# Two attention blocks with their gradients: head groups of four instead of five, with their out and dx products spread over 26 ticks

## The chip, the cores and the metric

The kernel runs on one core of one Trainium2 chip. The metric is the device time of one execution in microseconds; lower is better. The kernel before was timed three times: 1642.14, 1643.09 and 1643.6 us, so the median is 1643.09 us. Besides its time, an execution leaves a profile: a record of every instruction on the engines TensorE (PE; its weight loads are listed apart as PEld), VectorE (DVE), ScalarE (ACT), GpSimd (POOL) and SyncE (SP).

## What is computed

The reference runs two independent attention blocks A and B and concatenates their outputs; then it takes the gradient of all ten inputs for a given `grad_out`. The kernel returns the output and the ten gradients. One block is, with 8 batches of 96 queries, model width 640, 32 heads of 128, and 512 cached keys and values per batch and head, all bf16:

```python
q = (x @ wq).reshape(B, Sq, H, Dh).transpose(0, 2, 1, 3)
scores = jnp.einsum("bhqd,bhkd->bhqk", q, k_cache) * (Dh ** -0.5)
p = softmax(scores, axis=-1)
o = jnp.einsum("bhqk,bhkd->bhqd", p, v_cache)
out = o.transpose(0, 2, 1, 3).reshape(B, Sq, H * Dh) @ wo
```

For the change, two products matter. `out` is a sum over all 32 heads of (attention output of the head) times (that head's 128 rows of `wo`). The gradient `dx` is likewise a sum over heads of (gradient of the head's queries) times (that head's columns of `wq`, transposed). Both have 768 rows (8 x 96) and 640 columns.

## The kernel before, in words

**Ticks.** The work of block A and then of block B is cut into ticks: one tick for one batch of one head, so 8 ticks for a head, 256 for a block, 512 in all. `build_block` (line 54) does not emit instructions directly. It puts closures into a list with a tick and a slot (`em.add(tick, slot, fn)`), and at the end `Emitter.run` sorts the list by tick and slot and calls them. A scheduler below it takes the instructions in about this order and moves one only where a buffer or an input is not there yet. In the trace a tick can be found by its one product S_ps (L298).

**What a tick holds.** The stages of one batch of one head are spread over several ticks, so that a tick holds different stages of neighbouring batches (offsets in `OFF`, line 45): the scores S_ps (L298), their row maximum negm on VectorE (L300), the exponential E_sb on ACT (L310), its reciprocal row sum rinv (L320), P_sb on GpSimd (L329), four transposes of P and of dS (L365, L346), the attention output and the gradient of the queries into one bank x_ps (L359, L340), which ACT empties (OD, L375, and PT_sb, L378), and dV, dP and dK (L389, L417, L432), of which ACT empties dV and dK, and VectorE takes dP into dS (L421).

**What a head holds.** Once per head there are projections and weight gradients at fixed ticks of the head (`HK`, line 46): `pB` (L206 and after) transposes the head's slices of wo and wq on TensorE and copies them out as woT_h (ACT) and wqT_h (VectorE, L160); `pC` makes Q and dO (q_ps, L243); `pD` transposes them (n_ps, L258; dOnat_h and Qnat_h, L160); `qA` (nat_ps, L455), `qB` (dwo_ps, L469) and `qD` (dwq_ps, L490, once for two heads) make the gradients of wo and wq.

**What a group of heads holds.** The products for `out` and `dx` are made per group of heads: `gU` (L514) accumulates in one PSUM bank over the heads of the group, for one of 6 row tiles of 128 and one of two column pieces (512 and 128 wide), and then the bank is emptied. Here this is called a unit: 24 units for a group, 12 for `out` and 12 for `dx`, each with as many matmuls as the group has heads. The first group of a block writes its units into two f32 accumulators in SBUF, out_acc and dx_acc, by ACT (L157). All groups between add to them on VectorE (L518 for out, L520 for dx). The last group adds and writes the result as bf16, which is then stored.

**Where the units stand.** `cLg` is the last tick of the group. The 12 units of `out` begin 7 ticks after it and are spread evenly over `gs0` ticks; those of `dx` begin `gs0` + 7 ticks after it and are spread over `gs1`. Before, both are 9 for a group of five, 7 for a group of four, and 3 for the group of two. Block A has groups of 5, 5, 5, 5, 4, 4, 4 heads, block B of 5, 5, 5, 5, 5, 5, 2.

**Buffers that matter.** PSUM has one pool of 8 banks ("bank") for all tiles whose names end in `_ps`. wqT_h has 7 buffers (`HG` + 2, with `HG` = 5), and each is needed until the dx units of its group are done. OD, which holds the attention outputs and query gradients of the heads, has 7 places, and wo_h has 8 buffers.

Of the kernel before, what the change touches and what calls it, by code (L numbers as in the profile page):

```python
# [47 lines left out]
GSPREAD0 = 9  # L48
PRIO_OFF = 2000
GSPREAD1 = 9  # L50
# [3 lines left out]
def build_block(tc, em, tick0, blk, x, kc, vc, wq, wo, g_all, out_all, dx, dk, dv, dwq, dwo, ident, ones, pools, HG=6, first=True, groups=None):  # L54
# [12 lines left out]
    HG = min(HG, H)  # L67
    if groups is None:
        n_g = -(-H // HG)
        groups = [H // n_g + (1 if i < H % n_g else 0) for i in range(n_g)]  # L70
# [125 lines left out]
    def pA2(h):  # L196
        def f():
            wo_h = hst.tile([128, D], BF16, name="wo_h", bufs=HG + 3)
            ld = nc.sync.dma_start(wo_h[:], wo[h * 128:(h + 1) * 128, :])
            if not (first and h == 0):  # L200
                pinned(ld)
            HS[(blk, h)]["wo_h"] = wo_h
        return f
# [352 lines left out]
    def k_on_pe(h, b):  # L556
        return h == 0 or (first and h == 1)

    SX = pools["SX"]
    for g in range(NG):  # L560
        h0 = GH0[g]
        for hh in range(groups[g]):
            h = h0 + hh
            c0t = tick0 + h * B
            if not (first and h == 0):
                em.add(c0t + HK["pA"], SLOTS["LOAD"] + 1.7, pA(h))
                em.add(c0t + HK["pA2"], SLOTS["LOAD"] + 1.7, pA2(h))
            em.add(c0t + HK["pB"], SL_HEAD, pB(h))
            fh = first and h == 0
            p0, p1, d1, d0, late = HK["pC0"], HK["pC1"], HK["pD1"], HK["pD0"], 0  # L570
            if fh:
                p1, d1, d0, late = [3, 3], 3, 4, 7
            elif h == 0:
                p0, p1, d1, d0, late = [-2, 2], [0, 3], 3, 4, 7
            for si in range(NTS):
                em.add(c0t + p0[min(si, 1)], SL_HEAD, pC(h, 0, si))
                em.add(c0t + p1[min(si, 1)], SL_HEAD + late, pC(h, 1, si))
            em.add(c0t + d1, SL_HEAD + (8 if late else 0), pD(h, 1))
            em.add(c0t + d0, SL_HEAD, pD(h, 0))
            for b in range(B):  # L580
                ct = c0t + b
                if b % NB == 0:
                    em.add(tick0 - 12 if first and h == 0 and b == 0 else ct + OFF["ldk"], SLOTS["LOAD"], c_ld(h, b, "K", 7))
                    em.add(ct + OFF["ldv"], SLOTS["LOAD"], c_ld(h, b, "V", 6))
                    if not k_on_pe(h, b):
                        em.add(ct + OFF["kt"], SLOTS["LOAD"] + 1, c_xt(h, b, "KT", 4))
                    em.add(ct + OFF["vt"], SLOTS["LOAD"] + 1, c_xt(h, b, "VT", 4))
                if k_on_pe(h, b):
                    em.add(ct + 2, SLOTS["S1"], c_s1(h, b))
                em.add(ct + OFF["s2"], SLOTS["S2A"], c_s2a(h, b))  # L590
                em.add(ct + OFF["s2"], SLOTS["S2B"], c_s2b(h, b))
                em.add(ct + OFF["s3"], SLOTS["S3A"], c_s3a(h, b))
                em.add(ct + OFF["s3"], SLOTS["S3B"], c_s3b(h, b))
                em.add(ct + OFF["s5"], SLOTS["S5B"], c_s5b(h, b))
                if b % 2 == 1:
                    em.add(ct + OFF["s4"] + 1, SLOTS["LOAD"] + 1.5, c_st(h, b, "v"))
                    em.add(ct + OFF["s7"] + 1, SLOTS["LOAD"] + 1.5, c_st(h, b, "k"))
                em.add(ct + OFF["s4"], SLOTS["S4"], c_s4(h, b))
                for i, o in enumerate(("s8", "s7", "s5", "s4")):
                    SX.setdefault(ct + OFF[o], [None] * 4)[i] = (blk, h, b)  # L600
                em.add(ct + OFF["s6"], SLOTS["S6"], c_s6(h, b))
                em.add(ct + OFF["s7"], SLOTS["S7"], c_s7(h, b))
            hk = HK if first or h < H - 1 else dict(HK, qA0=13, qB=[14, 15], qA1=16, qD=[(19, 0, 2), (19, 2, 4), (19, 4, 5)])
            em.add(c0t + hk["qA0"], SL_HEAD, qA(h, 0))
            for di in range(len(wsplits)):
                em.add(c0t + hk["qB"][di], SL_HEAD + 1, qB(h, di))
            em.add(c0t + hk["qB"][-1] + 1, SLOTS["LOAD"] + 1.6, qB_st(h))
            em.add(c0t + hk["qA1"], SL_HEAD, qA(h, 1))
            for (k_, c_lo, c_hi) in hk["qD"]:
                if c_lo < DC and h % 2 == 1:  # L610
                    em.add(c0t + k_, SL_HEAD + 2, qD(h, c_lo, min(c_hi, DC)))
            if h % 2 == 1:
                em.add(c0t + hk["qD"][-1][0] + 1, SLOTS["LOAD"] + 1.6, qD_st(h))
        cLg = tick0 + (h0 + groups[g] - 1) * B + B - 1
        gs0 = max(3, (GSPREAD0 * groups[g]) // HG)
        gs1 = max(3, (GSPREAD1 * groups[g]) // HG)
        if not first and g == NG - 2:
            gs0, gs1 = 9, 9
        if g == 0:
            em.add(cLg + OFF["s5"] - 2, SL_LOAD, setup_acc)  # L620
        subs = [(0, t, gi) for t in range(TT) for gi in range(len(gsplits))] + [(1, t, gi) for t in range(TT) for gi in range(len(gsplits))]
        n_out = TT * len(gsplits)
        for i, (which, t, gi) in enumerate(subs):
            if which == 0:
                tk = cLg + OFF["s5"] + 2 + (i * gs0) // n_out
            else:
                tk = cLg + OFF["s8"] + 2 + gs0 - 3 + ((i - n_out) * gs1) // n_out
            em.add(tk, SL_GRP, gU(g, which, t, gi))
            if g == NG - 1 and gi == len(gsplits) - 1:
                em.add(tk + 1, SLOTS["LOAD"] + 1.6, gU_st(which, t))  # L630
# [3 lines left out]


def _kernel_impl(tc, A_x, A_k_cache, A_v_cache, A_wq, A_wo, B_x, B_k_cache, B_v_cache, B_wq, B_wo, grad_out,
           out_0, out_1, out_2, out_3, out_4, out_5, out_6, out_7, out_8, out_9, out_10, HG=5, slots=None, off=None, hk=None, ev=None, gspread=None, groupsA=None, groupsB=(5, 5, 5, 5, 5, 5, 2)):
    global GSPREAD0, GSPREAD1
    nc = tc.nc
    if slots:  # L640
        SLOTS.update(slots)
    if off:
        OFF.update(off)
    if hk:
        HK.update(hk)
    if ev:
        EV.update(ev)
    if gspread:
        GSPREAD0, GSPREAD1 = gspread
    with ExitStack() as ctx:  # L650
        P = lambda **kw: ctx.enter_context(tc.tile_pool(**kw))
        cst = P(name="gconst", bufs=1)
        ident = cst.tile([128, 128], BF16, name="ident")
        make_identity(nc, ident[:])
        ones = cst.tile([128, 1], BF16, name="ones")
        nc.vector.memset(ones[:], 1.0)
        warm = cst.tile([128, 128], BF16, name="warm")
        nc.vector.memset(warm[:], 1.0)
        pools = dict(
            const=P(name="const", bufs=1),  # L660
            ps=P(name="ps", bufs=8, space=PSUM),
            kvp=P(name="kv", bufs=11),
            wk=P(name="wk", bufs=3),
            hd=P(name="hd", bufs=2),
            hst=P(name="hst", bufs=HG + 2),
            grp=P(name="grp", bufs=1),
            stp=P(name="stp", bufs=5),
        )
        warm_ps = pools["ps"].tile([128, 128], F32, name="warm_ps", tag="bank")
        for _ in range(32):  # L670
            nc.tensor.matmul(warm_ps[:], warm[:], warm[:], start=True, stop=True)
        pools["SX"] = {}
        pools["XP"] = {}
        pools["OD"] = pools["const"].tile([128, 2, HG + 2, A_x.shape[0] * A_x.shape[1]], BF16, name="OD", bufs=1)
        pools["HS"] = {}
        pools["CS"] = {}
        em = Emitter()
        t_next = 13
        for blk, args in enumerate(((A_x, A_k_cache, A_v_cache, A_wq, A_wo, grad_out, out_0, out_1, out_2, out_3, out_4, out_5),
                                    (B_x, B_k_cache, B_v_cache, B_wq, B_wo, grad_out, out_0, out_6, out_7, out_8, out_9, out_10))):  # L680
            H_ = args[1].shape[1]
            if blk == 0:
                grps = groupsA
            else:
                grps = groupsB
            t_next = build_block(tc, em, t_next, blk, *args, ident, ones, pools, HG=HG, first=(blk == 0), groups=grps)
        for tk, (k8, k7, k5, k4) in pools["SX"].items():
            em.add(tk, SLOTS["S8"], pools["c_s8"](tk, k8, k7))
            em.add(tk, SLOTS["S5"], pools["c_s45"](tk, k8, k5, k4))
        em.run()  # L690
# [64 lines left out]
```

## Time and profile before

| | |
|---|---|
| time, median of 3 | 1643.09 us (1642.14 to 1643.6) |
| profiled execution: time, span | 1643.09 us, 1641.3 us |
| around the span | 1.8 us |
| TensorE clock granted | 1.000 |
| VectorE, GpSimd busy | 1268.2 us, 526.7 us |
| HBM traffic | 161.09 MB read, 159.12 MB written |
| matmul records | 21048 |
| group products (L514) | 1536 |

The span reaches from the first to the last instruction of the execution; the time has some 1.8 us around it. A row of a group of instructions reads: line, engine, operation, tile written and tiles read, shapes, count | busy us, mean ns of one | idle time of the engine just before them, and what ended it. A row of the waits reads: engine and line that waited, whom it waited for, us in total, number of times, the longest. A row of a timeline reads: start in us, length in us, instruction, and in brackets the idle time before it. Since matmuls overlap in the array, the length of a matmul's record (219 ns for 128 columns) is longer than its distance to the next one.

### The profile page before, as it was taken

To read this page: it belongs to the slowest core of one execution; us is meant where nothing else is said; L and a number is where in the kernel's file an instruction comes from. 1 tells how busy PE (TensorE), PEld (TensorE's weight loads), DVE (VectorE), ACT (ScalarE), POOL (GpSimd) and SP (SyncE) were. 2 spreads that over 40 slices of the span, in tenths; PEclk is the share of its full clock that TensorE was granted. 3 is DMA by queue.
4 is the path that set the end of the run, shared out by engine and by line. 5 is a ranking of instruction groups with operands and counts; after the bars stand their busy time and mean duration, and the time that the engine had idled before them with its cause. 6 is when DMAs were issued, how large, how long until landed. Compare 5 with 4: busy or idle time off the path is not lost.

```text
span 1641.3 us, 55280 instructions
## 1 busy us (share of the span) xinstructions
PE 1621.3 (99%) x21048; PEld 1289.1 (79%) x21048; DVE 1268.2 (77%) x2856; ACT 1388.7 (85%) x3518; POOL 526.7 (32%) x1034
## 2 busy tenths in 40 slices
PE   8999999999999999999999999999999999999999
PEld 7887787787787787877878877877877877877876
DVE  6886677778787787788878867878778778777777
ACT  7999897898798797988869998978977978987975
POOL 2333232333233232333323332323322322332332
PEclk9999999999999999999999999999999999999999
DMA  9999999999999999999999999999999999999994
GB/s 266 289 282 294 269 291 291 271 271 292 260 272 293 279 274 271 264 281 285 297 284 292 293 289 279 284 298 260 291 291 258 280 277 282 283 292 259 281 276 146
DMA packets 875626, 454.96 MB, mean 277 GB/s; under 512 B 548192, under 2 KB 875360, under 8 KB 875360
## 3 DMA queue, kind: packets, MB, share of 16 engines
q1 hardware_dynamic: 875360, 451.43, 112.4%
q8 instruction: 165, 2.70, 0.7%
q14 instruction: 101, 0.83, 0.1%
HBM read 161.09 MB, written 159.12 MB: 195 GB/s over the span
## 4 chain that ended last, share of the span: by engine, by line
PE 81%; ACT 10%; DVE 4%; issue 3%; DMA 2%; SPq 0%; POOL 0%; ACTq 0%; DVEq 0%; POOLq 0%
PE q_ps L243 13%; PE o_ps L514 12%; PE dwq_ps L490 6%; PE dP_ps L417 6%; PE dK_ps L432 6%; PE dV_ps L389 5%; PE S_ps L298 5%; PE dst_ps L346 5%; PE dwo_ps L469 4%; PE x_ps L365 4%; PE x_ps L359 4%; PE x_ps L340 4%; ACT E_sb L310 3%; ACT dK_sb L435 2%; PE n_ps L258 2%
## 5 line engine op out<-in xcount | busy, mean ns | idle before, releaser
L329 POOL TENSOR_SCALAR P_sb<-E_sb,rinv 96x512 bf16<-96x512 bf16 x512 | 352.5, 689 | 1087.9 <-DVE rinv L320 1053.6
L310 ACT ACTIVATE E_sb<-S_ps,negm 96x512 bf16<-96x512 f32 x512 | 354.8, 693 | 119.2 <-DVE negm L300 116.8
L421 DVE SCALAR_TENSOR_TENSOR dS_sb<-dP_ps,dl_ps,P_sb 96x512 bf16<-96x512 f32 x512 | 383.6, 749 | 48.9 <-PE dl_ps L419 40.2
L435 ACT ACTIVATE dK_sb<-dK_ps 128x512 bf16<-128x512 f32 x512 | 306.9, 599 | 97.5 <-PE dK_ps L432 96.5
L300 DVE TENSOR_REDUCE negm<-S_ps 96x1 f32<-96x512 f32 x512 | 347.7, 679 | 44.3 <-PE S_ps L298 42.1
L392 ACT ACTIVATE dV_sb<-dV_ps 128x512 bf16<-128x512 f32 x512 | 315.8, 617 | 0.0
L378 ACT ACTIVATE PT_sb<-x_ps 128x384 bf16<-128x384 bf16 x512 | 257.5, 503 | 0.0
L514 PEld LDWEIGHTS <-OD 128*128 128x128 bf16 x1536 | 135.7, 98 | 103.3 <-issue 1.3
L389 PE MATMUL dV_ps<-dOnat_h,P_sb 96*128 96x128 bf16 x2048 | 197.9, 219 | 0.6 <-DVE dOnat_h L160 0.6
L432 PE MATMUL dK_ps<-Qnat_h,dS_sb 96*128 96x128 bf16 x2048 | 197.8, 219 | 0.0
L417 PE MATMUL dP_ps<-VT,dOT_h 128*96 128x512 bf16 x512 | 195.4, 382 | 0.7
L298 PE MATMUL S_ps<-KT,QT_h 128*96 128x512 bf16 x488 | 184.7, 379 | 3.9 <-ACT E_sb L310 2.7
L407 POOL TENSOR_TENSOR prod<-OD,dOT_h 128x96 bf16<-128x96 bf16 x512 | 185.6, 362 | 8.8 <-ACT OD L375 8.2
L348 DVE COPY dST_sb<-dst_ps 128x384 bf16<-128x384 bf16 x512 | 177.2, 346 | 14.0 <-PE dst_ps L346 13.2
L320 DVE RECIPROCAL rinv<-rowsum 96x1 f32<-96x1 f32 x512 | 80.0, 156 | 138.8 <-ACT E_sb L310 134.8
L346 PE MATMUL dst_ps<-ident,dS_sb 96*128 96x96 bf16 x2048 | 171.8, 206 | 4.3 <-ACT PT_sb L378 3.6
L375 ACT ACTIVATE OD<-x_ps 128x192 bf16<-128x192 f32 (+1 forms) x515 | 172.5, 335 | 3.4 <-PE x_ps L340 3.4
L359 PE MATMUL x_ps<-PT_sb,V_sb 128*128 128x96 bf16 x2048 | 172.2, 206 | 0.5 <-ACT PT_sb L378 0.5
L365 PE MATMUL x_ps<-ident,P_sb 96*128 96x96 bf16 x2048 | 171.7, 205 | 0.6 <-POOL P_sb L329 0.3
L340 PE MATMUL x_ps<-dST_sb,K_sb 128*128 128x96 bf16 x2048 | 170.7, 206 | 0.0
L340 PEld LDWEIGHTS <-K_sb 128*128 128x128 bf16 x2048 | 133.7, 98 | 37.1
L514 PE MATMUL o_ps<-wo_h,OD 128*128 128x128 bf16 (+1 forms) x768 | 141.0, 299 | 0.0
(75 smaller groups left out, 3051.9 us busy)
## 6 DMA issues: line engine op xcount, KB each, us to landing
out_dram<-dV_sb SPq DMA_DIRECT2D x256, 256.0 KB, 3.9
out_dram<-dK_sb SPq DMA_DIRECT2D x256, 256.0 KB, 3.6
K_sb<-in_A_k_cache_dram SPq DMA_DIRECT2D x128, 256.0 KB, 4.1
V_sb<-in_A_v_cache_dram SPq DMA_DIRECT2D x128, 256.0 KB, 4.1
K_sb<-in_B_k_cache_dram SPq DMA_DIRECT2D x128, 256.0 KB, 4.2
V_sb<-in_B_v_cache_dram SPq DMA_DIRECT2D x128, 256.0 KB, 4.0
out_dram<-dwo_sb SPq DMA_DIRECT2D x64, 160.0 KB, 3.2
out_dram<-dwq_sb SPq DMA_DIRECT2D x32, 320.0 KB, 3.8
```

Source lines behind the costliest of these rows:

```text
L298: nc.tensor.matmul(S_ps[:], hs["QT_h"][:, tok], st["KT"], start=True, stop=True)
L300: nc.vector.tensor_reduce(negm[:], S_ps[:], axis=AX.X, op=ALU.max, negate=True)
L310: nc.scalar.activation(E_sb[:], st["S_ps"][:], ACT.Exp, bias=st["negm"][:], scale=1.0, accum_out=rowsum[:])
L329: pinned(nc.gpsimd.tensor_scalar(P_sb[:], st["E_sb"][:], st["rinv"][:], 0.0, op0=ALU.mult, op1=ALU.add))
L340: nc.tensor.matmul(dQT_ps, st["K_sb"][:, c, :], st["dST_sb"][:, c * Sq:(c + 1) * Sq], start=(c == 0), stop=(c == KC - 1))
L389: nc.tensor.matmul(dV_ps[:, c * 128:(c + 1) * 128], P_sb[:, c * 128:(c + 1) * 128], hs["dOnat_h"][:, b * 128:(b + 1) * 128], start=True, s ...
L392: nc.scalar.activation(SB[(blk, h, b // 2, "v")][:, b % 2], dV_ps[:], ACT.Identity, scale=1.0)
L417: nc.tensor.matmul(dP_ps[:], hs["dOT_h"][:, tok], st["VT"], start=True, stop=True)
L421: nc.vector.scalar_tensor_tensor(dS_sb[:], dP_ps[:], dl_ps[:, 0:1], st["P_sb"][:], op0=ALU.subtract, op1=ALU.mult)
L432: nc.tensor.matmul(dK_ps[:, c * 128:(c + 1) * 128], dS_sb[:, c * 128:(c + 1) * 128], hs["Qnat_h"][:, b * 128:(b + 1) * 128], start=True, s ...
L435: nc.scalar.activation(SB[(blk, h, b // 2, "k")][:, b % 2], dK_ps[:], ACT.Identity, scale=1.0)
L514: nc.tensor.matmul(o_ps[:], src[:, t * 128:(t + 1) * 128], rhs, start=(hh == 0), stop=(hh == groups[g] - 1))
```

## The change

Block A is cut into eight groups of four heads, and block B into 5, 5, 4, 4, 4, 4, 4, 2. The units of a group of four are spread over 13 and 13 ticks (the one but last group of block B keeps 9 and 9, as before), those of a group of five over 9 and 9, those of the group of two over 3 and 3. `HG` stays 5, so all buffers stay as they are. The matmuls are the same in number and shape except that each unit of a group of four accumulates over four heads.

```diff
         cLg = tick0 + (h0 + groups[g] - 1) * B + B - 1
-        gs0 = max(3, (GSPREAD0 * groups[g]) // HG)
-        gs1 = max(3, (GSPREAD1 * groups[g]) // HG)
+        gs0, gs1 = {2: (3, 3), 4: (13, 13)}.get(groups[g], (9, 9))
         if not first and g == NG - 2:
             gs0, gs1 = 9, 9
...
-           out_0, out_1, out_2, out_3, out_4, out_5, out_6, out_7, out_8, out_9, out_10, HG=5, slots=None, off=None, hk=None, ev=None, gspread=None, groupsA=None, groupsB=(5, 5, 5, 5, 5, 5, 2)):
+           out_0, out_1, out_2, out_3, out_4, out_5, out_6, out_7, out_8, out_9, out_10, HG=5, slots=None, off=None, hk=None, ev=None, gspread=None, groupsA=(4,) * 8, groupsB=(5, 5, 4, 4, 4, 4, 4, 2)):
```

## The prediction

> **What bounds the kernel now.** I read the busy rows first, then the chain of work that ended last.
>
> ```profile
> PE 1621.3 (99%) x21048; PEld 1289.1 (79%) x21048; DVE 1268.2 (77%) x2856; ACT 1388.7 (85%) x3518; POOL 526.7 (32%) x1034
> ...
> PE 81%; ACT 10%; DVE 4%; issue 3%; DMA 2%; SPq 0%; POOL 0%; ACTq 0%; DVEq 0%; POOLq 0%
> ```
>
> TensorE is never idle for long, and 81% of the chain is its own work; ACT, the next, has 10%. But matmuls overlap, so busy time does not tell how much of it is lost. For that I took from the trace the distance from each matmul's start to the next one's. Its median is nearly constant for a form: 216 ns for 512 columns, 56 ns for 128, 42 to 43 ns for 96. What exceeds the median of the same tile and form I call lost: 54.1 us in all. The other 1587 us of the 1641.3 us span are nearly all matmul work, which the change moves but does not add to. So at stake is the 54.1 us, less jitter: the quietest of the 511 stretches between two S_ps products (one per tick, numbered from 0) still show some 19.5 ns each, 10 us in all.
>
> Where is the rest lost? In the timeline of TensorE two places look like this:
>
> ```profile
> 205.40 0.30 PE L469 MATMUL dwo_ps<-g_nat,Onat 128*128 128x320 bf16 x1
> 205.86 0.38 PE L298 MATMUL S_ps<-KT,QT_h 128*96 128x512 bf16 x1 [0.16 <-ACT E_sb L310]
> ...
> 300.84 0.39 PE L389 MATMUL dV_ps<-dOnat_h,P_sb 96*128 96x128 bf16 x4
> 301.33 0.42 PE L417 MATMUL dP_ps<-VT,dOT_h 128*96 128x512 bf16 x1
> ```
>
> First: a 320-column product, 0.135 us long by its median, is followed 0.46 us later, because ACT's exponential came late: 0.32 us lost. This is in a tick without group products. Second: four 56 ns products take 0.49 us, 0.27 us too long. Here dP_ps waited until VectorE had emptied dOnat, so for a PSUM bank. This is in a tick with dx products.
>
> By stretches, without the 19.5 ns of jitter: **(a)** the 283 stretches without group products hold most of it. At the same places of the 16 ticks of a head pair they lose the same each time, by number modulo 16: 0.197 us at 15, 0.318 at 0, 0.329 at 3, often 0.195 at 6 and 0.1 to 0.17 at 7. **(b)** In the out half of a group of five nothing is lost. **(c)** In its dx half it is 0.97 us: 0.44 and 0.26 in two stretches that hold two products each, 0.13 in one, the rest in crumbs of 0.035. **(d)** The three groups of four that end the first block (7+7 ticks) lose almost nothing while they run.
>
> The reason for (a) is in busy time by stretch of time, first a group of four, then ticks without:
>
> ```profile
> core 0: us, PE busy (x) PEld busy (x) DVE busy (x) ACT busy (x) POOL busy (x), PEclk, DMA share, GB/s
> 610.30:665.00 54.70, 54.53 (x674) 41.80 (x672) 43.82 (x100) 41.40 (x106) 16.00 (x32) 1.00 1.10 260
> 665.00:702.50 37.50, 37.29 (x520) 31.03 (x517) 29.34 (x67) 35.65 (x92) 13.57 (x27) 1.00 1.19 279
> ```
>
> ACT is busy 35.65 of 37.5 us (95%) without group products and 76% with them. Group products are TensorE work that costs ACT nothing; in their ticks ACT catches up.
>
> The reason for (c) is a wait that VectorE shows nine times:
>
> ```profile
> DVE wqT_h L160 <- PE o_ps L514: 3.7, 9, 0.4
> ```
>
> There are 7 buffers of wqT_h. Where the head seven later comes before the dx products of the group are done, its transposes (pB) wait in PSUM. In the built order of before this happens in nine groups of five: one bank of eight is taken for 10 stretches, a second for 3. (d) has no such wait, and no loss.
>
> **The change, part by part.** *It moves* TensorE work only: 1536 group products before and after. In the built order 228 stretches have some before, 361 after. Before, up to 10 products of five heads (two units) fall in one stretch; after, a group of four gives one unit to each of 24 ticks, 32 ticks apart. A pair of units (512 and 128 columns) is 4 x (216 + 56) = 1.09 us, so 0.54 us per tick against 0.907 (5 x 272 x 12 over 18).
>
> *It adds* VectorE work: 16 groups instead of 14, each 24 evictions, and all added ones add to the accumulators: 48.
>
> ```profile
> L520 DVE SCALAR_TENSOR_TENSOR dx_acc<-o_ps,dx_acc 128x512 f32<-128x512 f32 x60 | 41.4, 690 | 30.6 <-PE o_ps L514 30.5
> ...
> L520 DVE SCALAR_TENSOR_TENSOR dx_acc<-o_ps,dx_acc 128x128 f32<-128x128 f32 x60 | 16.6, 277 | 0.0
> ```
>
> 24 x (690 + 277) = 23.2 us, so VectorE goes from 1268 to 1291 us, 79% of the span. The cover is its 373 us of idle time. Per group tick it gets 0.48 us more than its base of 2.2 us (1268 less 240 adds at 0.48 us, over 512), 2.7 of about 3.2 us, 84%. If that cover were gone, the bounds are 0 and the 23.2 us; I take 0 on its own, and its effect on banks below.
>
> *Stretches without products.* After a group of four only 7 are left out of 32, at 12, 13, 14, 15, 0, 1, 2 of 16, and the next group's first product comes behind the place of loss at 3. From (a): 0.197 + 0.318 + 0.329 = 0.84 us per group.
>
> *The dx halves.* By the built order of after, 14 groups hold a bank (9 stretches, a second one 2), always at the phase of (c). Bounds: nothing, as in (d), and 0.97 us, as in (c). The two stretches with two units lost 0.70 of the 0.97; they now have one, as where 0.035 to 0.15 was lost. I take 0.5 us.
>
> The Trainium skill (Perfetto Trace Analysis, Matmul Optimizations) asks that all 8 PSUM banks be used; that speaks against this change, and (b) against (c) agrees with it. By that rule alone the longer holding, 154 stretches against 117, would cost the full 0.97 us per group, which is the second case below.
>
> *First group of block one.* Its evictions are on ACT (24 of 0.28 to 0.60 us, 10.6 us). ACT's average of 2.67 us per tick (1388.7 less 21 us, over 512) becomes 3.11 in 3.2, as tight as in (a). 24 ticks at (a)'s mean excess, 0.1 us or less, give 0 to 2.4; I take 1.5 us.
>
> *Queues.* SP's stores of block one's out and dx move to other ticks; each waits for VectorE (3.8 us in four waits now). Behind them on SP stand K and V loads that are issued four to five ticks ahead, over 12 us, so nothing. wqT_h copies that wait: 14 x 0.41 us on VectorE instead of 9, inside its idle time. Nothing moves on POOL. The end: the last but one group has four heads, so 9 products fewer (1.2 us) follow the last S_ps; they are done earlier, no gain.
>
> *The sum*, lost time without jitter:
> - stretches 32 to 255: 15.4 now; after 7 x (0.84 + 0.5) + 1.5 = 10.9; -4.5
> - 256 to 287 (block start, whose own waits stay): 2.7, after about 2.2; -0.5
> - 288 to 367, two groups of five: unchanged
> - 368 to 495: 9.2; after 4 x 1.34 = 5.4; -3.8
>
> Together -8.8 us. The profiled execution took 1643.09 us (span 1641.3 and 1.8 around it), which is also the median of the runs. Forecast: **1634.3 us**.
>
> **Rivals.** *Full price for held banks.* The dx half loses 0.97 us as before, in every group. Then 7 x 1.81 + 1.5 = 14.2, the block start 2.7, 4 x 1.81 = 7.2: -3.2 us, **1640 us**. For: the phase is the same, and a smaller PE share per tick leaves ACT less time. Against: losses sit in the two-unit stretches. 0.2.
>
> *Slower: VectorE late.* A tick now has only 0.54 us of group products to cover 0.48 us of adds; before 0.907 to cover 0.64. If VectorE's adds then hold o_ps banks and delay negm in every group tick, the out halves lose 0.97 us too: 11 x (0.84 + 1.94) + 1.5 + 3.7 = 35.8 against 27.3: +8.5, **1652 us**. It decides from where the two halves together lose 1.3 us per group ((27.3 - 1.5) / 12 - 0.84). For: ACT already waits for negm.
>
> ```profile
> ACT E_sb L310 <- DVE negm L300: 116.8, 190, 2.1
> ```
>
> Against: (b) and (d) lose nothing with denser adds. 0.15.
>
> *No loss in the dx halves*, as in (d), and none in the first group: -8.8 - 6 - 1.5, **1627 us**. For: one unit per tick. 0.1.
>
> *It moves nothing* because ACT's lag is only made up elsewhere: 1643 us. Against: (a) repeats to some ns at fixed places. 0.05. That the products don't spread is excluded by the built order.
>
> **How the numbers follow.** The forecast has 0.5 and 1629 to 1639 as its own range. The measurement of this kernel tells about 0.2% (3.3 us) from no change. Faster: 0.5 + 0.1 and a third of the 0.2 that falls below 1639.8, so 0.66. Same: the rest of that and 0.05, so 0.19. Slower: 0.15. The range leaves out the VectorE case and reaches from the case without loss to beyond full price, with the first group's 2.4: 1626 to 1646.
>
> **What would show it.** Right: TensorE's busy time and products as before, VectorE near 1291 us; lost time near 45 us; the losses at 6 and 7 gone and those at 15, 0, 3 once per group of four; wqT_h waiting 14 times. Wrong: matmul gaps behind out_acc or negm in out halves (VectorE case), or 0.2 to 0.4 us gaps at dP_ps, dwq_ps and S_ps in every dx half (bank case).

## The result and the profile after

The changed kernel takes 1646.08 us (median of 17 runs, 1645.5 to 1647.11) against 1642.92 us (17 runs) for the kernel before on the same chips: ratio 1.0019, interval 1.0012 to 1.0027. It is slower by 3.2 us. The forecast was 1634.3 us, and 1646.08 lies just outside the range of 1626 to 1646. The profiled execution took 1646.16 us with a span of 1644.4 us.

The first two lines of the page that answer to those shown of before, busy time and the shares of the chain of work:

```profile
PE 1614.1 (98%) x20850; PEld 1287.4 (78%) x21048; DVE 1295.0 (79%) x2904; ACT 1393.2 (85%) x3518; POOL 528.5 (32%) x1034
...
PE 81%; ACT 10%; DVE 4%; issue 4%; DMA 1%; POOL 0%; SPq 0%; ACTq 0%; DVEq 0%; POOLq 0%
```

The picture is that of before: TensorE bounds. VectorE has 48 instructions more and 26.8 us more work. One number misleads: 20850 matmuls against 21048. The 21048 weight loads are all there, and the built program has as many matmuls as before; 198 matmul records are missing from this trace, 133 of o_ps and 65 of q_ps, all 512 columns wide. Whoever takes distances from start to start must put them back at 216 ns each first, or counts 42.8 us of work as lost. I matched the records to the program's order. Then the work, each matmul at the median of its form, is 1587.2 us in both kernels, and the lost time is **53.1 us before and 56.1 us after**: 3.0 of the 3.2 us. (Here a form is told apart by its inputs too; by the tile written alone, as in the prediction, the 53.1 us are 54.1.)

By stretches between two S_ps, without 19.5 ns of jitter each, in us:

| stretches | before | forecast | after |
|---|---|---|---|
| 32 to 63 (first group in after) | 2.2 | 2.8 | 1.8 |
| 64 to 255 | 12.7 | 8.0 | 15.7 |
| 256 to 287 | 2.6 | 2.2 | 3.0 |
| 288 to 367 (unchanged groups of five) | 6.2 | 6.2 | 5.3 |
| 368 to 495 | 8.9 | 5.4 | 9.5 |

A middle group of four repeats every 32 stretches, at most places to a few nanoseconds. Its parts (mean of four groups, stretches 96 to 223) are what the study is about:

| part, number of the stretch modulo 32 | forecast | after |
|---|---|---|
| without products, and the first one (29 to 3) | 0.84 | 0.92 |
| out half (4 to 16) | 0 | 0.75 |
| dx half (17 to 28) | 0.5 | 0.75 |

The ticks without products cost about what was forecast, and look as before. First busy time in a group's 25 ticks and then without products, then the place where a 320-column product is followed 0.46 us later:

```profile
core 0: us, PE busy (x) PEld busy (x) DVE busy (x) ACT busy (x) POOL busy (x), PEclk, DMA share, GB/s
307.70:390.80 83.10, 81.88 (x1038) 64.70 (x1049) 66.01 (x147) 68.03 (x173) 25.77 (x51) 1.00 1.13 280
390.80:411.00 20.20, 19.80 (x283) 16.38 (x283) 17.21 (x40) 19.66 (x52) 8.00 (x16) 1.00 1.11 265
```

```profile
403.85 0.30 PE L469 MATMUL dwo_ps<-g_nat,Onat 128*128 128x320 bf16 x1
404.31 0.38 PE L298 MATMUL S_ps<-KT,QT_h 128*96 128x512 bf16 x1 [0.16 <-ACT E_sb L310]
```

ACT is 97% busy without products, 82% with them. VectorE has 79% in the group's ticks; no engine beside TensorE is full there. The waits:

```profile
ACT E_sb L310 <- DVE negm L300: 139.3, 212, 2.0
...
DVE wqT_h L160 <- PE o_ps L514: 5.4, 14, 0.5
```

wqT_h waits in 14 groups, as the built order said. And ACT waits 22.5 us longer for negm. The new loss stands in the out half, at the ticks numbered 7 modulo 8 (0.34 us at 7, 0.44 at 15). Timelines of TensorE, VectorE and ACT there:

```profile
321.17 0.38 PE L298 MATMUL S_ps<-KT,QT_h 128*96 128x512 bf16 x1
...
322.68 0.38 PE L417 MATMUL dP_ps<-VT,dOT_h 128*96 128x512 bf16 x1
323.10 0.17 PE L419 MATMUL dl_ps<-ones,prod 128*96 128x1 bf16 x1
323.27 0.50 PE L455 MATMUL nat_ps<-ident,OD 128*128 128x128 bf16 x6
```

```profile
321.21 0.54 DVE L160 COPY dQnat<-nat_ps 128x768 bf16<-128x768 bf16 x1
321.68 0.68 DVE L300 TENSOR_REDUCE negm<-S_ps 96x1 f32<-96x512 f32 x1
322.27 0.68 DVE L160 COPY dOnat_h<-n_ps 96x1024 bf16<-96x1024 bf16 x1
```

```profile
322.45 0.68 ACT L310 ACTIVATE E_sb<-S_ps,negm 96x512 bf16<-96x512 f32 x1 [0.82 <-DVE negm L300]
```

From S_ps to nat_ps TensorE has 1.76 us of products, by their medians, and takes 2.10. Only three narrow products of `out` (168 ns) are among them. It waits twice, each time for a PSUM bank; which tile takes over which bank stands in the built program. dl_ps takes over the bank of n_ps, which VectorE empties into dOnat_h. That copy stands behind dQnat and negm and ends at 322.95; dl_ps starts 0.15 us later and is 0.19 us late. nat_ps takes over the bank of S_ps itself, which is free when E_sb ends, at 323.13; nat_ps starts 0.14 us later and is another 0.15 us late. The second wait sets the whole: had dl_ps come in time, nat_ps would still have started at 323.27. (At 15 there are the same two waits, and 0.10 us before the next S_ps, for ACT's dK_sb.)

How much of it is VectorE's queue? VectorE is on dQnat (0.54 us) when S_ps comes, so negm is late. But E_sb ends 1.96 us after the start of S_ps here, and in the whole trace never sooner than 1.88, but for one tick with 1.82. So dQnat ahead of negm makes up some 0.08 of the 0.34 us. The rest is that the bank of S_ps is wanted after 1.76 us of work.

### The profile page after: what moved, and what is told of

Its sections match the earlier page's. It is cut to its first block, busy times and chain, and to the rows that moved or that the text cites. A ratio compares the mean times of both kernels' runs of the same rounds, so it can differ in the third digit from the quotient of the medians.

```text
span 1644.4 us, 55072 instructions
## 1 busy us (share of the span) xinstructions
PE 1614.1 (98%) x20850; PEld 1287.4 (78%) x21048; DVE 1295.0 (79%) x2904; ACT 1393.2 (85%) x3518; POOL 528.5 (32%) x1034
## 4 chain that ended last, share of the span: by engine, by line
PE 81%; ACT 10%; DVE 4%; issue 4%; DMA 1%; POOL 0%; SPq 0%; ACTq 0%; DVEq 0%; POOLq 0%
PE q_ps L243 12%; PE o_ps L514 11%; PE dwq_ps L490 6%; PE dK_ps L432 6%; PE dV_ps L389 5%; PE dP_ps L417 5%; PE S_ps L298 5%; PE dwo_ps L469 5%; PE dst_ps L346 5%; PE x_ps L365 4%; PE x_ps L359 4%; PE x_ps L340 4%; ACT E_sb L310 3%; PE n_ps L258 2%; PE nat_ps L455 2%
## 5 line engine op out<-in xcount | busy, mean ns | idle before, releaser
L514 PEld LDWEIGHTS <-OD 128*128 128x128 bf16 x1536 | 140.2, 98 | 104.4 <-issue 3.2
L514 PE MATMUL o_ps<-wo_h,OD 128*128 128x128 bf16 (+1 forms) x706 | 148.9, 292 | 3.3
```

The source lines that it names most:

```text
L514: nc.tensor.matmul(o_ps[:], src[:, t * 128:(t + 1) * 128], rhs, start=(hh == 0), stop=(hh == groups[g] - 1))
```

## The experiments

**Theories.** *Bank*: in the dx halves the transposes of wq that wait for a wqT_h buffer hold a PSUM bank, and that is what TensorE waits for. *VectorE queue*: in the out halves copies or adds ahead of negm on VectorE make it, and with it the exponential, late. *Cover* (rival to the queue): the new units are too thin at that place, whatever VectorE does, so a bank is wanted before the exponential has freed it. *Adds* (the prediction's slower rival): the 48 added adds are what costs. *ACT*: the loss without products comes from ACT alone.

All kernels were timed beside the kernel before on the same chip.

| kernel | us | ratio to before (interval) | out / dx / without, us per group |
|---|---|---|---|
| after | 1646.08 | 1.0019 (1.0012 to 1.0027) | 0.75 / 0.75 / 0.92 |
| e1_narrow_first | 1643.86 | 1.0001 (0.9992 to 1.0010) | 0.52 / 0.74 / 0.88 |
| e2_small_adds | 1641.21 | 0.9990 (0.9981 to 0.9999) | 0.66 / 0.39 / 0.88 |
| e3_wqT9 | 1637.09 | 0.9962 (0.9950 to 0.9975) | 0.75 / 0.16 / 0.88 |
| e4_spread7 | 1640.10 | 0.9977 (0.9968 to 0.9986) | other ticks |
| e5_before_wqT9 | 1636.74 | 0.9960 (0.9948 to 0.9973) | groups of five |
| e6_wqT9_narrow | 1635.57 | 0.9951 (0.9939 to 0.9964) | 0.53 / 0.16 / 0.88 |
| e7_wqT8 | 1637.99 | 0.9967 (0.9954 to 0.9979) | 0.75 / 0.16 / 0.88 |
| e8_wqT9_qA16 | 1638.54 | 0.9971 (0.9960 to 0.9982) | 0.46 / 0.03 / 1.20 |
| e9_narrow_Onat_dve | 1632.71 | 0.9934 (0.9920 to 0.9949) | 0.59 / 0.20 / 0.69 |
| e10_before_Onat_dve | 1641.13 | 0.9990 (0.9980 to 0.9999) | groups of five |

**The bank: e3, e7, e5.**

```diff
-            wqT_h = hst.tile([128, D], BF16, name="wqT_h")
+            wqT_h = hst.tile([128, D], BF16, name="wqT_h", bufs=9)
...
-            stp=P(name="stp", bufs=5),
+            stp=P(name="stp", bufs=4),
```

> The changed kernel with 9 instead of 7 buffers of wqT_h (and 4 instead of 5 of the staging tile, to make room): no transposes of wq wait in PSUM for the dx products, so no bank is held for 9 ticks. Bank theory: the dx halves lose nothing instead of 0.71 us per group, 14 groups: some 8 us less, 1637 to 1640 us, and the out halves still lose 0.78 us. If the dx halves lose for the same reason as the out halves, and the held bank matters little: 1644 to 1647 us.

Measured: 1637.09 us, 9.0 below the changed kernel. The dx half loses 0.16 instead of 0.75 us per group and the out half 0.75 as before; no wait of wqT_h is left among the waits. What is left in the dx half, 0.18 us at 23, is nat_ps waiting for a bank that the wide add of dx frees. The dose, `bufs=8` on the changed kernel with the staging tile as it was:

> The changed kernel with 8 buffers of wqT_h and the staging tile as it was (5): the head seven later no longer waits, the head eight later still does, for 2 stretches instead of 9 + 2. Bank theory: of the 0.71 us per dx half the 0.2 us at the stretches 26 to 28 of 32 may stay, and the rest goes: 1638 to 1641 us, 6 to 8 us below the changed kernel. If the 9.0 us came from the staging tile: 1645 to 1647 us.

1637.99 us; the dx half loses 0.16 us here too. So the two stretches that a bank is still held cost nothing to be seen, the staging tile is not the cause, and the long holding is. Then the same edit as e3 on the kernel before:

> The kernel before (groups of five) with 9 buffers of wqT_h and 4 of the staging tile. Bank theory: the nine dx halves that lost 0.97 us while a bank was held lose little, 6 to 9 us less than the kernel before: 1634 to 1637 us. If the changed kernel gained from the buffers for another reason (its units are thinner), 1641 to 1643 us.

1636.74 us, 6.4 below the kernel before. The bank theory stands. It also shows what the change is worth when no bank is held: 0.9962 against 0.9960, nothing that these runs can tell.

**The out half: e1, e2, e8.** e1 changes the order of the out units in the middle groups:

```diff
-        subs = [(0, t, gi) for t in range(TT) for gi in range(len(gsplits))] + [(1, t, gi) for t in range(TT) for gi in range(len(gsplits))]
+        subs = [(0, t, gi) for t in range(TT) for gi in ((1, 0) if 0 < g < NG - 1 else (0, 1))] + [(1, t, gi) for t in range(TT) for gi in range(len(gsplits))]
```

> The changed kernel, with the out units of the middle groups in the order narrow (128), wide (512) instead of wide, narrow. Nothing else moves: so in the out half a wide unit (0.86 us) instead of a narrow one (0.22 us) now stands at the ticks whose number modulo 8 is 7, where the changed kernel loses 0.35 and 0.44 us per group. Cover theory (the exponential's bank is wanted again too soon where only a narrow unit lies between): these two losses fall to 0.1 us or less each, 6 to 8 us in all, so about 1639 us. VectorE theory (its adds delay negm, wherever they stand): the wide add of 0.69 us now falls into those ticks, and the losses stay or grow: 1646 to 1650 us.

1643.86 us, 2.2 below the changed kernel. The loss at 7 falls from 0.34 to 0.19 and that at 15 from 0.44 to 0.18, but 0.18 us appears at 16. Timelines of TensorE, VectorE and ACT at 7:

```profile
320.27 0.38 PE L298 MATMUL S_ps<-KT,QT_h 128*96 128x512 bf16 x1
...
322.49 0.16 PE L419 MATMUL dl_ps<-ones,prod 128*96 128x1 bf16 x1
322.71 0.49 PE L455 MATMUL nat_ps<-ident,OD 128*128 128x128 bf16 x6
```

```profile
320.32 0.54 DVE L160 COPY dQnat<-nat_ps 128x768 bf16<-128x768 bf16 x1
320.78 0.68 DVE L160 COPY dOnat_h<-n_ps 96x1024 bf16<-96x1024 bf16 x1
321.38 0.68 DVE L300 TENSOR_REDUCE negm<-S_ps 96x1 f32<-96x512 f32 x1
321.98 0.68 DVE L518 TENSOR_TENSOR out_acc<-o_ps,out_acc 128x512 f32<-128x512 f32 x1
```

```profile
322.15 0.69 ACT L310 ACTIVATE E_sb<-S_ps,negm 96x512 bf16<-96x512 f32 x1 [1.04 <-DVE negm L300]
```

dl_ps should last 26 ns to the next start and lasts 220; the add ends at 322.66, and nat_ps starts 50 ns later. Neither theory holds. negm starts 1.11 us after S_ps here, against 0.51 in the changed kernel, and E_sb ends only at 322.84, after nat_ps has started. So the thicker cover (2.25 us of products from S_ps to nat_ps) hides nothing; nat_ps simply does not need that bank. In this built program it takes over the bank of the wide product, which the wide add empties. And dOnat_h now runs ahead of negm, so that dl_ps, which takes over its bank as before, does not wait.

e2 cuts the adds of the middle groups to 8 columns:

```diff
             def add(dst):
-                if which == 0:
+                if 0 < g < NG - 1:
+                    nc.vector.tensor_tensor(acc[:, t, c0:c0 + 8], o_ps[:, 0:8], acc[:, t, c0:c0 + 8], op=ALU.add)
+                elif which == 0:
```

> The changed kernel, with the out evictions of the middle groups cut to 8 columns (out is then not summed; dx is). This takes some 0.2 to 0.6 us from each of 156 adds on VectorE, and nothing from TensorE. VectorE theory: the losses in the out halves (0.78 us per group, 11 or 12 groups) go, 1636 to 1639 us. Cover theory: the losses stay within a third, since S_ps, negm and the exponential take as long as before: 1643 to 1646 us.

The edit did more than the expectation says: it cut the evictions of dx too (144 of each), so neither out nor dx is summed over the middle groups here. Measured: 1641.21 us, 4.9 below the changed kernel. In the out half 0.34 us at 7 stays and 0.44 at 15 falls to 0.34: 0.09 us per group. In the dx half 0.36 us goes, where a bank is held. So 79 us less work on VectorE (1216.2 us busy instead of 1295.0) is worth less than the bank (9.0 us), and the out half keeps most of its loss, by the same two waits: the adds are not its main cause. Next, with 9 buffers, the transposes of dQ one tick earlier:

```diff
-HK = dict(pA=-10, pA2=-9, pB=-3, pC0=[-2, 0], pC1=[-1, 0], pD1=1, pD0=2, qA0=18, qA1=17, qB=[19, 20], qD=[(18, 0, 2), (19, 2, 4), (21, 4, 5)])
+HK = dict(pA=-10, pA2=-9, pB=-3, pC0=[-2, 0], pC1=[-1, 0], pD1=1, pD0=2, qA0=18, qA1=16, qB=[19, 20], qD=[(18, 0, 2), (19, 2, 4), (21, 4, 5)])
```

> As the changed kernel with 9 buffers of wqT_h, and the transposes of dQ (nat_ps, whose copy dQnat takes 0.54 us of VectorE) one tick earlier, so that dQnat no longer stands just ahead of dOnat and negm on VectorE. Queue theory (in the out halves negm comes late because dQnat, dOnat and an add stand ahead of it, and with it the exponential that frees the next bank): the 0.34 and 0.44 us per group in the out halves fall to 0.1 or less, and the 0.18 in the dx halves too, 7 to 10 us: 1627 to 1630 us. If the loss is set by TensorE having too little work between S_ps and the next bank, whatever VectorE does: it stays within 2 us of 1637 us.

On VectorE the tick now runs without dQnat, and dOnat_h stands ahead of negm. VectorE, then TensorE and ACT:

```profile
322.94 0.75 DVE L421 SCALAR_TENSOR_TENSOR dS_sb<-dP_ps,dl_ps,P_sb 96x512 bf16<-96x512 f32 x1 [0.28 <-PE dl_ps L419]
323.61 0.68 DVE L160 COPY dOnat_h<-n_ps 96x1024 bf16<-96x1024 bf16 x1
324.20 0.68 DVE L300 TENSOR_REDUCE negm<-S_ps 96x1 f32<-96x512 f32 x1
```

```profile
323.25 0.38 PE L298 MATMUL S_ps<-KT,QT_h 128*96 128x512 bf16 x1
...
325.08 0.16 PE L419 MATMUL dl_ps<-ones,prod 128*96 128x1 bf16 x1
325.14 0.49 PE L455 MATMUL nat_ps<-ident,OD 128*128 128x128 bf16 x6
```

```profile
324.98 0.68 ACT L310 ACTIVATE E_sb<-S_ps,negm 96x512 bf16<-96x512 f32 x1
```

The losses at 7 and 15 fall from 0.34 and 0.44 to 0.13 each, and that at 23 from 0.18 to 0.04. The queue theory holds for one of the two waits: dOnat_h is done at 324.29, 0.79 us before dl_ps, which takes over its bank here too. It fails for the other, the one it was made for: negm starts 0.95 us after S_ps, later than in the changed kernel, and E_sb ends at 325.66, but nat_ps starts at 325.14 all the same. In this built program it takes over the bank of dK_ps, free at 325.09. New losses come a tick or two later, 0.18 us at 16, 0.17 at 1 and 0.21 at 2, at the transposes of P, which wait for GpSimd's P_sb, and at 2 at that of dS, which waits for VectorE. The time is 1638.54 us, not less than e3. The forecast gain of 7 to 10 us fails: the loss moved.

The out half of a group of five in the kernel before shows the same from the other side. TensorE, then ACT:

```profile
396.79 0.38 PE L298 MATMUL S_ps<-KT,QT_h 128*96 128x512 bf16 x1
...
398.58 0.16 PE L419 MATMUL dl_ps<-ones,prod 128*96 128x1 bf16 x1
398.61 0.49 PE L455 MATMUL nat_ps<-ident,OD 128*128 128x128 bf16 x6
```

```profile
398.49 0.67 ACT L310 ACTIVATE E_sb<-S_ps,negm 96x512 bf16<-96x512 f32 x1
```

From S_ps to nat_ps there are four narrow products of `out` instead of three, 1.82 us of work, and nothing is lost. That is not the 56 ns of cover: E_sb ends at 399.16, half a microsecond after nat_ps has started. dl_ps and nat_ps take over the banks of two products of `out`, free since 397.63 and 398.42, and the bank of S_ps is next taken over by the next S_ps, at 399.60. So at these ticks it is the bank which the next products take over that decides, more than the thickness of a unit or a late negm.

**The parts of the change: e4.**

```diff
-        gs0, gs1 = {2: (3, 3), 4: (13, 13)}.get(groups[g], (9, 9))
+        gs0, gs1 = {2: (3, 3), 4: (7, 7)}.get(groups[g], (9, 9))
```

> The groups of four without the wider spread (7 and 7 ticks, as the groups of four had before): dx is done before the wqT_h buffer is wanted, no bank is held. If what the three groups of four of the kernel before showed (about 1.7 us lost per 32 ticks, all of it in ticks without products) holds for all of them, 12 x (2.3 - 1.7) = 7 us less than the changed kernel: about 1639 us, 4 us below the kernel before; the 48 added adds then cost nothing. If the added adds are what costs, it is as slow as the changed kernel or slower: 1645 to 1650 us.

1640.10 us, as expected: the cut into groups of four, with its 48 adds, is 3.5 us *faster* than the kernel before on the same chip (1643.58 us there). The spread over 26 ticks (with the banks that it holds) then costs 6.0 us against e4; the intervals of the two ratios, 0.9977 and 1.0019, lie apart. The adds alone cost nothing here.

**The best of both: e6, e9, e10.** e6 is e3 and e1 together.

> The changed kernel with both: 9 buffers of wqT_h and the out units narrow first. If bank holding and the VectorE queue at the ticks numbered 7 modulo 8 are two separate causes, the gains add up: 9.0 + 2.3 us below the changed kernel, about 1635 us. If they are one cause, no more than the buffers alone: 1637 us.

1635.57 us: 1.5 us below e3 by the medians, and in the profile the out half loses 0.53 instead of 0.75 us per group, as in e1, beside the dx half's 0.16. So bank and order add up per stretch; as times, the intervals of e3 and e6 overlap. e9 moves the copy Onat from ACT to VectorE on top of e6, e10 does it on the kernel before:

```diff
-EV = dict(pB0="act", pB1="dve", pC00="act", pC01="act", pC10="act", pC11="dve", pD0="dve", pD1="dve", qA0="act", qA1="dve", qB0="act", qB1="dve", qD="dve", gU="act")
+EV = dict(pB0="act", pB1="dve", pC00="act", pC01="act", pC10="act", pC11="dve", pD0="dve", pD1="dve", qA0="dve", qA1="dve", qB0="act", qB1="dve", qD="dve", gU="act")
```

> The changed kernel with 9 buffers of wqT_h and narrow first, and the copy Onat (64 times 0.82 us) on VectorE instead of ACT. ACT theory for the ticks without group products (they lose because ACT is 95% busy there): the 0.23, 0.32 and 0.34 us per group at 31, 0 and 3 of 32 shrink to half or less, 5 to 8 us, against something lost to a fuller VectorE: 1629 to 1633 us. If VectorE's queue is what sets the pace everywhere: 0.5 us more per head on VectorE makes it slower than 1635.6, 1638 to 1645 us.

> The kernel before with the copy Onat on VectorE instead of ACT, nothing else. ACT theory: the ticks without group products, which lose some 23 us over the kernel beside the 10 us of jitter, lose half of it: 1630 to 1637 us. Queue theory: 1643 to 1650 us.

e9: 1632.71 us, the lowest median here, 10 us below the kernel before and well below the changed one (its interval still overlaps that of e6). In its profile the losses at 0 and 3 fall from 0.32 and 0.34 to 0.18 and 0.14, that at 31 hardly changes, and 0.17 us appears at 2, behind P_sb. So ACT is a cause, but where it is relieved the chain by VectorE and GpSimd comes next. On the kernel before the gain is 0.10% (0.9990), at the edge of what the runs tell and far below the forecast of 6 to 13 us.

## Why the prediction was wrong

- **Bound and stake**: right. TensorE's work is the same (1587.2 us), and the difference in time is the difference in lost time.
- **Stretches without products**, 0.84 us per group: right (0.92, and 0.88 in e1, e2, e3, e6 and e7). The losses at 6 and 7 without products went, but the ticks numbered 7 modulo 8 now lose more with products.
- **"In the out half of a group of five nothing is lost", carried over to groups of four at one unit per tick**: this step failed. The out half of a middle group loses 0.75 us, 8 us over 11 groups. What the runs show in its place are two waits for a PSUM bank in one tick per head: dl_ps takes over the bank that dOnat_h empties, third in VectorE's queue (0.19 us), and nat_ps the bank of S_ps, after 1.76 us of work, while S_ps, negm and E_sb need at least 1.88 (0.15 us more). In groups of five the same products, with 1.82 us of work, take over other banks. The prediction compared VectorE's and ACT's load averaged over ticks (84%) and counted banks held in the dx halves; which tile takes over which bank in the out halves it did not ask, and the new schedule changed that.
- **dx half, "I take 0.5 us"**: the mechanism was right (e3, e7, e5) and the size too small: 0.75 us, 3 us over 12 groups. The held bank cost 9.0 us in the changed kernel and 6.4 in the one before. One unit per tick is no cure while a bank is missing. The rule of the Trainium skill that spoke against the change (Perfetto Trace Analysis, Matmul Optimizations: use all 8 PSUM banks) agrees with these runs; giving the bank back is worth more than anything the change moves.
- **First group**, 1.5 us dearer: wrong sign. Stretches 32 to 63 lose 1.8 us, less than a middle group's 2.4. ACT's evictions fitted.
- **48 adds, 23.2 us of VectorE**: right in size (26.8 us measured over all of VectorE) and nothing on their own (e4).
- **The slower rival** (both halves at full price, 1652 us, deciding from 1.3 us for both halves together): the halves lose 1.5 us together, just beyond that point, and the kernel is slower by a little. Its place was right. Its cause was not: the added adds cost nothing on their own (e4), and with the adds cut to 8 columns the out half still loses 0.66 of its 0.75 us (e2).

That the first group loses little in its out half (0.08 us at 7, where a middle group loses 0.34) fits: its nat_ps takes over the bank of n_ps, not that of S_ps.

Open: by what rule the pool hands out the banks, so that a change of the schedule alters which product follows S_ps in its bank. The waits are read from the built programs and the traces; no run here changed a bank and nothing else, and the new losses of e8 and e9 were followed no further than to the wait that ended them.

## What to carry to other kernels

When a bound engine runs without gaps to be seen, take its lost time from start to start, fold it on the period of the schedule, and look at each place by itself: averages by engine hide a tick in which three long copies meet. For each place that loses, find the bank that the late product takes over and what empties it: a new schedule also hands out the banks anew, and a loss that goes or comes may be that alone. And before moving work, look for a buffer whose wait holds a PSUM bank: here one or two more buffers of 1.25 KB per partition were worth two to three times the 3.2 us by which the change slowed the kernel.

## What the runs showed of the hardware

The loss repeats at most of its places to a few ns over hundreds of us. A matmul that waited for a bank started 0.05 us after the end of the copy that freed it (nat_ps behind the wide add in e1) or 0.14 to 0.15 us after it (nat_ps behind E_sb and dl_ps behind dOnat_h in after). What does not repeat is K's transposing DMA: in stretches 288 to 340 (within the second block) S_ps waited for it 1.2 us in the profile of before (0.74 and 0.43), 2.7 us in e4 (1.50 and 1.17), and not at all in after and e6. So a single profile differs from another by a microsecond or two for this alone, and the gain in stretches 288 to 367 of the table, where nothing was changed, is mostly that. Matmul records can be missing in number (198 here), all of 512 columns, while the weight loads are complete.
